# Sparse attention with a multiplicative feed-forward: w3 loaded ahead of batch 1, batch 1's phases in a new order, four stores on another queue

## Chip, cores and metric

The kernel runs on one core of one Trainium2 chip. The metric is the device time of one execution in microseconds (us). A profile of one further execution shows every instruction of the core's engines: PE (matrix products; PEld loads its weights), DVE, ACT and POOL (elementwise work), and SP, which here only issues transfers. Of these only PE, DVE, ACT and POOL compute.

## What is computed

`setup_inputs` draws q, k, v of 8 batches, 8 heads, 576 positions and 64 channels, and four weights; all are float32. Heads 0 to 3 attend to the last 32 positions, heads 4 to 7 to every 32nd position before. The result is projected twice, multiplied, and projected twice more.

```python
def _attn_ref(q, k, v):
    ...
    scores = scale * np.matmul(q, k.transpose(0, 1, 3, 2))
    ...
    mask_local = (rel >= 0) & (rel < stride)
    mask_strided = (rel >= 0) & (pos[None, :] % stride == pos[:, None] % stride)
    ...
    attn = attn / (np.sum(attn, axis=-1, keepdims=True) + 1e-09)
    return np.matmul(attn, v).astype(np.float32)

def _moe_ref(x, w1, w2, w3, w_out):
    a = x @ w1
    b = x @ w2
    h = a * b @ w3
    return (h @ w_out).astype(np.float32)
```

x has 4608 rows (8 times 576) and 512 columns; w1 and w2 are 512x1024, w3 1024x1024, w_out 1024x512.

## The kernel before

**Attention.** The 64 heads are 32 pairs, four to a batch: p0 to p3 are batch 0, p4 to p7 batch 1, p8 to p11 batch 2. Pairs 0 and 1 of a batch are local, 2 and 3 strided. A pair goes through these phases: T (PE transposes its q and k, ACT or DVE copy them from PSUM to `qT` and `kT`), S (scores on PE, exp on ACT, mask product on DVE), PV (product with v on PE, then `norm` on DVE: a reciprocal and a product), T2 (PE transposes the result, ACT and DVE copy it to `xT`). Batches 0 and 1 use the functions that begin with `ah_`, in two halves (groups 0 and 1) of a pair; later batches use `ph_`. `ah_R` transposes the last 64 positions of all pairs of a batch, and its second part (the tail) copies q's part for the strided pairs. Strided pairs of batches 0 and 1 have their probabilities in a large buffer `nptm`, which has to be cleared first (`nptm1` for batch 1), and a small DVE copy (`ah_tail`, L434) behind each mask product (`mask_mul`, L343).

**Feed-forward.** Rows are cut into nine tiles of 512. `ab_parts` makes a, b and their product for a tile (L585, L594, L597), `o_parts` the product with the folded weight (L635), whose result ACT copies to `osb` (L646, three buffers) and stores (L647). w3 and w_out are folded on the chip into `w34`: `fold_tr(jc)` transposes the jc-th 128 rows of w3 (L677), `fold_mm(jc)` multiplies them with w_out in two halves. Batch 1's last part of attention stands among these: 31 units are issued one after the other, and `plan` says behind which unit a phase of batch 1 is put. Units 1 to 23 are the fold (unit 14 is fold_tr(5), 15 and 16 the second half of fold 4 and the first of fold 5, 17 fold_tr(6), 18 and 19 halves of folds 5 and 6, 20 fold_tr(7), 21 to 23 halves of folds 6, 7 and 7), 24 to 31 the halves of tile 0's four products, each pair of which ends in a store. Then come the parts of tile 1 that belong to batch 0's last 64 rows (`over_parts`), and the loop over tiles, in which the later batches' attention is spread.

**Order of the work.** PE's instructions run in the order of the code. The other engines' and the queues' order is set when the kernel is built, from priorities in the order of the code and a model of when each instruction can start, so it can differ from the code's. All loads are issued by SyncE, all stores but one by ACT. Each load goes to one of nine staging buffers (`stgp`) and is then cast to float16 by POOL, so a load waits for the cast of the ninth load before it. The transposed pieces of w3 lie in six buffers (`w3n`): the seventh and eighth piece wait for fold_tr(0) and fold_tr(1). `load_vL` loads v of the local pairs in two halves (four transfers, L221, casts L222 and copies L91), `load_vN` and `load_vX` that of the strided pairs; `load_rest` the last 64 positions of q and k (L209); `load_qk(b, grp)` q and k of two pairs (L199).

**PSUM** has eight banks: psF three, psB two times two (`sps`, `pt`, `xps`), psM one, used by R, T2 and, before the change, by T of batch 1's local pairs. T of p6 and p7 takes two banks of psF.

Of the kernel before, what the change touches and what calls it, by code (L numbers as in the profile page):

```python
# [19 lines left out]
def kernel(  # L20
# [11 lines left out]
    nc = tc.nc  # L32
# [4 lines left out]
    P = 128  # L37
    NT = 512
    NTILE = NTOK // NT
    KM = DM // P  # L40
    KF = DF // P
# [33 lines left out]
    def pe(ins):  # L75
        return tc.keep_in_program_order(ins)
# [3 lines left out]
    def behind(ins):  # L80
        return tc.issue_after(ins.ins) if ins is not None else nullcontext()
# [4 lines left out]
    def copy(eng, out, in_):  # L86
        if eng == "a":
            return nc.scalar.copy(out=out, in_=in_)  # L88
        elif eng == "v":
            return nc.vector.tensor_copy(out=out, in_=in_)  # L90
        return nc.gpsimd.tensor_copy(out=out, in_=in_)  # L91
# [72 lines left out]
    out_r = out.rearrange("(c p) n -> c p n", p=P)  # L164
# [12 lines left out]
    def load_w3(jc, eng):  # L177
        st = stgp.tile([P, DF], FP32, tag="stg")
        nc.sync.dma_start(st, moe_w3[bass.ds(jc * P, P), :])
        t = ffn.tile([P, DF], FP16, tag="w3n", bufs=6)  # L180
        w3n[jc] = t
        copy(eng, t, st)
# [13 lines left out]
    def load_qk(b, grp, engs="pp"):  # L196
        for nm, ten, eng in (("q", q, engs[0]), ("k", k, engs[1])):
            st = stgp.tile([P, 4, 4, D], FP32, tag="stg")
            nc.sync.dma_start(st.rearrange("p h c d -> p h (c d)"),  # L199
                              ten[b, 4 * grp:4 * grp + 4, 0:NM].rearrange("h (p c) d -> p h (c d)", c=4))  # L200
            t = qkp.tile([P, 4, 4, D], FP16, tag=f"{nm}{grp}")
            with behind(setup["p"] if b == 0 and grp == 0 else None):
                copy(eng, t, st.rearrange("p h c d -> p c h d"))
            x16[(b, nm, grp)] = t
# [52 lines left out]
    for b in range(B):  # L257
        for hp in range(4):
            s = Pair()
# [107 lines left out]
    def ah_T1(s, i, dst=None):  # L367
        if dst is None:
            dst = psF.tile([P, 2 * NM], FP16, tag="f", name="tps")[:, 0:NM]
        src = x16[(s.b, "qk"[i], s.hp // 2)]  # L370
        h0 = 2 * (s.hp % 2)
        for c in range(4):
            pe(nc.tensor.transpose(dst[:, c * P:(c + 1) * P],
                                   src[:, c, h0:h0 + 2].rearrange("p h d -> p (h d)"), id16))
        return dst

    def ah_T1c(s, i, dst):
        t = (qT, kT)[i]
        eng = "v" if i and (s.b == 0 or not s.local) else "a"
        if s.local:  # L380
            copy(eng, t[:, s.hp, 0:NM].rearrange("x (p c) -> x p c", c=4),
                 dst.rearrange("x (c p) -> x p c", c=4))
        elif i:
            copy(eng, t[:, s.hp, 0:NM], dst)
        else:
            copy(eng, t[:, s.hp].rearrange("x (c w) -> x c w", w=NW)[:, :, 0:P],
                 dst.rearrange("x (c p) -> x c p", c=4))
# [2 lines left out]
        ah_T1c(s, i, ah_T1(s, i))  # L390

    def ah_T(s):
        if s.b and s.local:
            ps = psM.tile([P, 2, NM], FP16, tag="m", name="tps")
            pst = [ah_T1(s, i, ps[:, i]) for i in range(2)]
        else:
            pst = [ah_T1(s, i) for i in range(2)]
        for i in range(2):
            ah_T1c(s, i, pst[i])

    def ah_R(b):
        ps = psM.tile([P, 1024], FP16, tag="m", name="rps")
        pvs = [ps[:, 256 * i:256 * i + 256].rearrange("x (g a w) -> x g a w", g=2, a=2) for i in range(2)]
        src = x16[(b, "r")]
        for g in range(4):
            pe(nc.tensor.transpose(pvs[g // 2][:, g % 2].rearrange("x a w -> x (a w)"),
                                   src[:, 2 * g:2 * g + 2].rearrange("p h d -> p (h d)"), id16))
        for i, t in enumerate((qT, kT)):
            copy("av"[i], t[:, 0:2, NM:S], pvs[0][:, :, i])
        copy("v", kT[:, 2:4, NM:S], pvs[1][:, :, 1])  # L410

        def tail():
            copy("a" if b else "v", qT[:, 2:4].rearrange("x g (c w) -> x g c w", w=NW)[:, :, :, P:NW],
                 pvs[1][:, :, 0].rearrange("x g (j c) -> x g c j", c=4))

        return tail

    def ah_home(s):
        if s.nat:
            return nptms[s.b][:, s.hp - 2], NE  # L420
        return ptms[s.hp % 2], PTW

    def ah_off(s, g):
        return g * (640 if s.local else 2 * QN[2])
# [12 lines left out]
    def ah_group(s, g):  # L437
        m = s.n // 2
        e = s.n if g else m
        return range(g * m, e), s.q[g * m], s.q[e]  # L440
# [55 lines left out]
    def ah_PV(s, g):  # L496
        cs, lo, hi = ah_group(s, g)
        ptm, end = ah_home(s)
        if s.b == 0:
            xps = psF.tile([P, NB], FP32, tag="f", name="xpl")[:, 0:390].rearrange("p (h x) -> p h x", h=2)  # L500
        else:
            xps = psB.tile([P, 2, NB], FP32, tag="big", name="xps")
        for i, c in enumerate(cs):
            for h in range(2):
                c0 = ah_off(s, g) + h * (hi - lo) + s.q[c] - lo
                m = min(P, end - c0)
                o = xps[0:m, h, i * 65:(i + 1) * 65]
                tail = s.nat and c == NC
                pe(nc.tensor.matmul(o, ptm[0:s.kr, c0:c0 + m],
                                    s.v[0:s.kr, 2 * (s.hp % 2) + h, c, :], start=True, stop=not tail))  # L510
                for e in range(NC if tail else 0):
                    e0 = NE + h * 256 + e * 64
                    pe(nc.tensor.matmul(o, ptm[:, e0:e0 + P], s.v[:, 2 * (s.hp % 2) + h, e, :],
                                        start=False, stop=e == NC - 1))
        if g == 0:
            s.xqs = att.tile([P, LT, 2, D], FP16, tag="xqs", bufs=2, name="xqs")
        norm(s, xps[0:s.kr, :, 0:len(cs) * 65], cs[0], len(cs))

    def norm(s, xv, c0, l):
        w = s.kr  # L520
        rcp = att.tile([P, 2, LT], FP32, tag="rcp")
        xv = xv.rearrange("p h (i e) -> p h i e", e=65)
        nc.vector.reciprocal(out=rcp[0:w, :, 0:l], in_=xv[:, :, :, D])
        nc.vector.tensor_mul(s.xqs[0:w, c0:c0 + l].rearrange("p i h d -> p h i d"), xv[:, :, :, 0:D],  # L524
                             _ap(rcp, 0, [[rcp.ap[0][0], w], [LT, 2], [1, l], [0, D]]))
# [115 lines left out]
    def o_parts(tch):  # L641
        res = []
        for ts in range(NT // P):
            def done(ps, ts=ts):
                osb = ffn.tile([P, DM], FP32, tag="osb", bufs=3)
                nc.scalar.copy(out=osb, in_=ps)  # L646
                nc.scalar.dma_start(out_r[tch * (NT // P) + ts], osb)  # L647

            if tch + 1 < NTILE or ts + 1 < NT // P:
                res += acc_parts(lambda ci, ts=ts: abts[tch][:, ci, bass.ds(ts * P, P)],  # L650
                                 lambda ci: w34[:, ci, :], done, 4)
        return res
# [49 lines left out]
    def ph_TS(s, t):  # L702
        if s is not None:
            pt, soft = ph_S(s)
            after = [soft]
        else:
            pt = psB.tile([P, 2, NB], FP32, tag="big", name="pt")
            after = []
        if t is not None:
            after.append(ph_T(t, t.hp == 0, pt))  # L710
        for f in after:
            f()
# [116 lines left out]
    load_w3(0, "p")  # L829
    for g in range(4):  # L830
        load_wo(g, "p")
    for jc in range(1, 6):
        load_w3(jc, "p")
    load_qk(1, 0)
    load_w3(6, "p")
    load_rest(1)
    load_w3(7, "p")
    load_vL(1)
    load_qk(1, 1)
    load_vN(1)  # L840

    while pos[0] < batch_end[0]:
# [18 lines left out]
    p4, p5, p6, p7, p8 = pairs[4:9]  # L861
    def nptm1():
        nptms.append(ffn.tile([P, 2, 2048], FP16, tag="abt", bufs=4, name="nptm1"))
        clear(nc.vector, nptms[1])

    plan = ((24, nptm1), (15, ah_T, p4), (18, lambda: ah_R(1)()), (19, ah_T, p5), (20, ah_S, p4), (22, ah_S, p5),
            (23, ah_PV, p4, 0), (24, ah_PV, p4, 1), (25, ah_PV, p5, 0), (25, ph_T2, p4), (26, ah_PV, p5, 1),
            (26, ah_T, p6), (27, ah_T, p7), (28, ah_S, p6), (28, ph_T2, p5), (29, ah_S, p7), (30, ah_PV, p6, 0),
            (31, ah_PV, p6, 1), (31, ah_PV, p7, 0))
    for i, u in enumerate(units, 1):  # L870
        u()
        for x in plan:
# [4 lines left out]
    load_vX(2)  # L877
    over = over_parts()
    tile1 = ab_parts(1) + o_parts(1)
    for u in over[0:3]:  # L880
        u()
    ph_T2(p6)
    over[3]()
    ah_PV(p7, 1)
    over[4]()
    ph_TS(None, p8)
    for u in over[5:]:
        u()
    tile1[0]()
# [56 lines left out]
```

## Time and profile before

| what | value |
|---|---|
| median of 3 runs | 278.85 us (275.86, 278.85, 280.79) |
| profiled execution | 277.33 us, span 275.6 us from the first to the last instruction |
| PE / DVE / ACT / POOL busy | 259.7 / 150.4 / 146.7 / 100.3 us |
| PE's granted clock | 0.998 |
| moved by DMA | 48.66 MB, 177 GB/s in the mean |

Busy times are sums over the span and don't add up, since engines work at the same time. A line of a timeline has the start, the length, the engine, the line of the kernel, the operation and its tiles, and in square brackets the idle time of that engine just before it with what ended it. "ACTq" and "SPq" are the issuing of transfers by ACT and SyncE. A line of waits has who waited for whom, the sum in us, how often, and the longest.

### The profile page before, as it was taken

Reading aid. Unit: us, or ns where it says so; the run is one execution under the profiler, and the core shown is the slowest. Engines: PE = TensorE matmul, PEld = TensorE weight load, DVE = VectorE, ACT = ScalarE, POOL = GpSimd, SP = SyncE. Lnnn points to the kernel's source line nnn. Section 1 sums busy time; section 2 is a strip of 40 time slices with the busy share of each in tenths; the row PEclk is TensorE's granted clock in tenths of the full one; section 3 lists DMA queues with packets and bytes.
Section 4 is the critical chain, followed back from the end, with each engine's and each line's share of the span. In section 5 each row is a group of like instructions: output and inputs, shape, how many; then the busy total and the mean of one; then the engine's idle time right before and its main releaser. Section 6 shows DMA issues by size and latency. Waiting matters only on the chain.

```text
span 275.6 us, 6430 instructions
## 1 busy us (share of the span) xinstructions
PE 259.7 (94%) x2508; PEld 138.3 (50%) x2508; DVE 150.4 (55%) x340; ACT 146.7 (53%) x304; POOL 100.3 (36%) x119
## 2 busy tenths in 40 slices
PE   2989999987789999999999999999999999999995
PEld 1654445543645555555555555555555544444442
DVE  7483533483877547755775576467547752431430
ACT  2754334737356765657555565656665664324322
POOL 5577785765446533557248275200000000000000
PEclk9999999999999999999999999999999999999999
DMA  7999999998599749499596994210021012003004
GB/s 213 289 353 394 394 386 249 252 247 249 188 234 229 218 159 273 135 244 305 150 263 188 288 236 146 100 54 4 2 114 40 0 40 114 0 4 150 0 1 153
DMA packets 61099, 48.66 MB, mean 177 GB/s; under 512 B 31804, under 2 KB 52492, under 8 KB 61068
## 3 DMA queue, kind: packets, MB, share of 16 engines
q1 hardware_dynamic: 55884, 38.87, 51.1%
q10 hardware_dynamic: 5184, 9.37, 9.0%
q8 instruction: 19, 0.31, 0.5%
q14 instruction: 12, 0.10, 0.1%
HBM read 38.80 MB, written 9.44 MB: 175 GB/s over the span
## 4 chain that ended last, share of the span: by engine, by line
PE 76%; DMA 10%; DVE 5%; ACT 3%; SPq 2%; issue 1%; ACTq 1%; POOL 1%; POOLq 0%
PE ops L635 23%; PE aps L585 20%; PE bps L594 19%; DMA st<-in_moe_w_dram 8%; PE sps L363 3%; PE ps L533 3%; DMA st<-in_v_dram 2%; PE sps L329 2%; PE pt L286 2%; DVE ptm L343 1%; PE pt L329 1%; PE trp L677 1%; ACT qT L88 1%; ACTq L647 1%; SPq L199 1%
## 5 line engine op out<-in xcount | busy, mean ns | idle before, releaser
L594 PE MATMUL bps<-xT,w2h 128*128 128x512 f16 (+1 forms) x288 | 74.7, 376 | 0.0
L585 PE MATMUL aps<-xT,w1h 128*128 128x512 f16 (+1 forms) x288 | 73.6, 377 | 0.5 <-ACT xT L540 0.5
L635 PE MATMUL ops<-w,abt 128*128 128x512 f16 x280 | 67.0, 379 | 0.0
L597 DVE TENSOR_TENSOR abt<-bps,asb 128x512 f16<-128x512 f32 (+1 forms) x72 | 48.8, 680 | 32.0 <-PE bps L594 29.6
L565 ACT COPY asb<-aps 128x512 f32<-128x512 f32 (+1 forms) x72 | 42.5, 593 | 43.0 <-PE aps L585 40.6
L91 POOL CAST t<-st 128x1024 f16<-128x1024 f32 (+1 forms) x46 | 48.2, 1055 | 33.1 <-DMA st<-in_k_dram 12.4
L585 PEld LDWEIGHTS <-w1h 128*128 128x128 f16 x288 | 26.4, 98 | 29.6 <-issue 1.0
L594 PEld LDWEIGHTS <-w2h 128*128 128x128 f16 x288 | 26.1, 98 | 26.4 <-issue 0.3
L635 PEld LDWEIGHTS <-abt 128*128 128x128 f16 x280 | 25.2, 98 | 26.0 <-issue 0.2
L354 ACT ACTIVATE pte<-sps 128x1024 f16<-128x1024 f32 (+1 forms) x24 | 24.6, 1026 | 11.4 <-PE sps L329 11.4
L646 ACT COPY osb<-ops 128x512 f32<-128x512 f32 x35 | 20.6, 589 | 17.2 <-PE ops L635 17.2
L524 DVE TENSOR_TENSOR xqs<-sps,rcp 128x768 f16<-128x768 f32 (+1 forms) x24 | 21.4, 891 | 0.8
L343 DVE TENSOR_TENSOR ptm<-pte,maskL 128x1152 f16<-128x1152 f16 (+2 forms) x16 | 12.9, 808 | 14.4 <-ACT pte L354 13.6
L88 ACT COPY qT<-pt 128x224 f16<-128x224 f16 (+4 forms) x60 | 18.0, 361 | 3.5 <-ACT osb L646 1.6
L343 DVE TENSOR_TENSOR ptm<-pte,maskX 126x1152 f16<-126x1152 f16 x12 | 10.2, 848 | 13.4 <-ACT pte L354 13.4
L222 POOL CAST v16L<-st 96x768 f16<-96x768 f32 x16 | 13.2, 824 | 10.0 <-DMA st<-in_v_dram 7.2
L545 ACT COPY xT<-ps 128x504 f16<-128x504 f16 x12 | 6.9, 578 | 18.3 <-PE ps L533 18.3
L250 POOL CAST v16X<-st 126x1024 f16<-126x1024 f32 x6 | 6.8, 1129 | 24.4 <-DMA st<-in_v_dram 17.6
L635 PE MATMUL ops<-woh,w3T 128*128 128x512 f16 x64 | 15.6, 380 | 0.0
L533 PEld LDWEIGHTS <-xqs 96*128 96x128 f16 (+3 forms) x176 | 11.5, 97 | 8.1 <-DVE xqs L524 1.9
L533 PE MATMUL ps<-id,xqs 96*128 96x96 f16 (+3 forms) x176 | 14.1, 210 | 1.2 <-DVE xqs L524 1.2
L90 DVE COPY kT<-pt 128x512 f16<-128x512 f16 (+4 forms) x48 | 14.1, 324 | 1.4 <-ACT kT L88 0.6
(114 smaller groups left out, 265.7 us busy)
## 6 DMA issues: line engine op xcount, KB each, us to landing
out_dram<-osb ACTq DMA_DIRECT2D x35, 256.0 KB
st<-in_q_dram SPq DMA_DIRECT2D x16, 512.0 KB
st<-in_k_dram SPq DMA_DIRECT2D x16, 512.0 KB
st<-in_moe_w_dram SPq DMA_DIRECT2D x16, 512.0 KB
st<-in_v_dram SPq DMA_DIRECT2D x32, 144.0 KB
st<-in_v_dram SPq DMA_DIRECT2D x24, 112.0 KB
st<-in_moe_w_out_dram SPq DMA_DIRECT2D x4, 512.0 KB
st<-in_q_dram SPq DMA_DIRECT2D x8, 128.0 KB
```

Of the source, the lines that this page charges most:

```text
L88: return nc.scalar.copy(out=out, in_=in_)
L91: return nc.gpsimd.tensor_copy(out=out, in_=in_)
L343: nc.vector.tensor_mul(o.rearrange("p (a x) -> p a x", x=x), i.rearrange("p (a x) -> p a x", x=x), _ap(s.mask, lo, [[s.mask.ap[0][0], s.kr ...
L354: nc.scalar.activation(out=pv[0:kr, :, lo:hi], in_=src, func=AF.Exp, bias=0.0, scale=scale)
L524: nc.vector.tensor_mul(s.xqs[0:w, c0:c0 + l].rearrange("p i h d -> p h i d"), xv[:, :, :, 0:D], _ap(rcp, 0, [[rcp.ap[0][0], w], [LT, 2], [ ...
L533: pe(nc.tensor.transpose(ps[:, o:o + l], s.xqs[0:l, t].rearrange("p h d -> p (h d)"), id16[0:l, 0:l]))
L565: nc.scalar.copy(out=st["asb"][:, 0:nt], in_=st["a"][:, 0:nt])
L585: pe(nc.tensor.matmul(st["a"][:, 0:nt], w1h[:, ci, bass.ds(jc * P, P)], xT[ci][:, tok], start=(ci == 0), stop=(ci == KM - 1)))
L594: pe(nc.tensor.matmul(st["b"][:, 0:nt], w2h[:, ci, bass.ds(jc * P, P)], xT[ci][:, tok], start=(ci == 0), stop=(ci == KM - 1)))
L597: nc.vector.tensor_mul(abts[tch][:, jc, skip:], st["b"][:, 0:nt], st["asb"][:, 0:nt])
L635: pe(nc.tensor.matmul(st["ps"], lhs(ci), rhs(ci), start=(ci == 0), stop=(ci == KF - 1)))
L646: nc.scalar.copy(out=osb, in_=ps)
```

## The change

It has four parts. (1) All eight pieces of w3 are loaded ahead of batch 1; both halves of batch 1's q and k come ahead of its v. (2) T of all pairs of batch 1 uses one bank of psM. (3) The phases of batch 1 have new places in `plan`, p6's and p7's T and p6's S ahead of PV of p4, and behind the units T of p8 comes first, ahead of the overflow parts and PV of p7's second half. (4) The four stores of tile 0 are issued by SyncE; in the code they stand ahead of `load_vL(2)`, `load_qk(2, 1)` and `load_vX(2)`.

```diff
     def ah_T(s):
-        if s.b and s.local:
+        if s.b:
             ps = psM.tile([P, 2, NM], FP16, tag="m", name="tps")
...
                 nc.scalar.copy(out=osb, in_=ps)
-                nc.scalar.dma_start(out_r[tch * (NT // P) + ts], osb)
+                (nc.scalar if tch else nc.sync).dma_start(out_r[tch * (NT // P) + ts], osb)
...
-    for jc in range(1, 6):
+    for jc in range(1, KF):
         load_w3(jc, "p")
     load_qk(1, 0)
-    load_w3(6, "p")
     load_rest(1)
-    load_w3(7, "p")
+    load_qk(1, 1)
     load_vL(1)
-    load_qk(1, 1)
     load_vN(1)
...
-    plan = ((24, nptm1), (15, ah_T, p4), (18, lambda: ah_R(1)()), (19, ah_T, p5), (20, ah_S, p4), (22, ah_S, p5),
-            (23, ah_PV, p4, 0), (24, ah_PV, p4, 1), (25, ah_PV, p5, 0), (25, ph_T2, p4), (26, ah_PV, p5, 1),
-            (26, ah_T, p6), (27, ah_T, p7), (28, ah_S, p6), (28, ph_T2, p5), (29, ah_S, p7), (30, ah_PV, p6, 0),
-            (31, ah_PV, p6, 1), (31, ah_PV, p7, 0))
+    plan = ((16, ah_T, p4), (18, lambda: ah_R(1)()), (19, ah_T, p5), (20, ah_S, p4), (21, ah_T, p6), (22, ah_S, p5),
+            (23, ah_T, p7), (23, nptm1), (24, ah_S, p6), (25, ah_PV, p4, 0), (25, ah_PV, p4, 1), (26, ah_PV, p5, 0),
+            (27, ah_S, p7), (27, ah_PV, p5, 1), (27, ph_T2, p4), (28, ph_T2, p5), (29, ah_PV, p6, 0),
+            (30, ah_PV, p6, 1), (31, ah_PV, p7, 0))
...
-    for u in over[0:3]:
+    ph_TS(None, p8)
+    over[0]()
+    ah_PV(p7, 1)
+    for u in over[1:4]:
         u()
     ph_T2(p6)
-    over[3]()
-    ah_PV(p7, 1)
     over[4]()
-    ph_TS(None, p8)
     for u in over[5:]:
```

## Prediction

> **What bounds the kernel now.** I read the page first, then PE's waits, then PE's busy time in stretches of the middle, then the timelines of ACT, POOL, DVE and SyncE there.
>
> ```profile
> PE 259.7 (94%) x2508; PEld 138.3 (50%) x2508; DVE 150.4 (55%) x340; ACT 146.7 (53%) x304; POOL 100.3 (36%) x119
> ...
> PE   2989999987789999999999999999999999999995
> ```
>
> PE is busy for 94% of the span. The only slices below 9 after the start are slices 9 to 11, about 55 to 76 us. After that PE is full to the end, so a microsecond saved before 78 us is a microsecond off the span, and none can be saved behind it. PE's busy time in stretches (length, PE, PEld, DVE, ACT, POOL):
>
> ```profile
> 46.00:52.00 6.00, 5.48 (x52) 3.46 (x50) 1.89 (x5) 3.45 (x8) 3.78 (x5) 1.00 1.05 205
> 52.00:58.00 6.00, 5.79 (x59) 2.78 (x56) 4.89 (x10) 4.33 (x9) 4.86 (x6) 1.00 1.04 321
> 58.00:64.00 6.00, 3.89 (x44) 2.51 (x45) 3.04 (x9) 2.42 (x5) 3.67 (x6) 1.00 0.88 176
> 64.00:71.00 7.00, 5.88 (x73) 2.91 (x72) 4.68 (x11) 4.40 (x8) 4.58 (x7) 1.00 0.89 282
> 71.00:77.50 6.50, 5.01 (x142) 4.09 (x138) 4.67 (x16) 2.87 (x9) 1.34 (x2) 1.00 0.41 130
> ```
>
> 31.5 us hold 26.05 us of PE work: 5.5 us idle, all that the change can win. A matmul's shown end overlaps the next one's start (four 128x512 show 1.03 us but follow each other every 0.86), so each of some six gaps hides about 0.1 more: I count 6.1 from start to start. PE's waits in that stretch say what ended them:
>
> ```profile
> PE tps L373 <- ACT qT L88: 1.8, 2, 1.3
> PE xps L509 <- DVE xqs L524: 1.8, 2, 1.0
> PE ps L533 <- DVE xqs L524: 1.0, 2, 0.8
> ```
>
> The 1.3 is batch 1's transposes of p7 at 63.26. They wait for the copy of p6's q, which stands on ACT behind a store's issue:
>
> ```profile
> 59.62 0.64 ACT L88 COPY xT<-ps 128x576 f16<-128x576 f16 x1 [1.21 <-PE ps L533]
> 59.98 2.60 ACTq L647 DMA_DIRECT2D out_dram<-osb  x1
> 62.63 0.58 ACT L88 COPY qT<-tps 128x512 f16<-128x512 f16 x1 [2.37 <-PE ops L635]
> ```
>
> The DVE waits are p4's to p7's softmax, norm and next bank of psB, one after the other, late because p6 and p7 begin only at 60.5. Batch 1's loads set how early they could begin (POOL's casts: w3's sixth, q, k of p4/p5, w3's seventh and eighth, k of p6/p7):
>
> ```profile
> 40.71 1.04 POOL L91 CAST t<-st 128x1024 f16<-128x1024 f32 x1 [0.26 <-DMA st<-in_moe_w_dram]
> 42.22 1.04 POOL L91 CAST t<-st 128x1024 f16<-128x1024 f32 x1 [0.47 <-DMA st<-in_q_dram]
> 44.24 1.04 POOL L91 CAST t<-st 128x1024 f16<-128x1024 f32 x1 [0.99 <-DMA st<-in_k_dram]
> 46.32 1.04 POOL L91 CAST t<-st 128x1024 f16<-128x1024 f32 x1 [1.04 <-DMA st<-in_moe_w_dram]
> ...
> 49.81 1.04 POOL L91 CAST t<-st 128x1024 f16<-128x1024 f32 x1 [1.47 <-PE rps L406]
> ...
> 55.98 1.58 POOL L91 CAST t<-st 128x1024 f16<-128x1024 f32 x1 [0.69 <-DMA st<-in_k_dram]
> ```
>
> **Loads.** No transfer is added; SyncE issues the same ones and POOL makes the same casts in another order. From 28 to 42 us DMA is full, and one 512 KB piece of w3 follows the other every 1.28 us (35.57 to 40.71 is four). So the two moved pieces come at 42.0 and 43.3. Their buffers are free: fold_tr(0) and (1) read the old ones at 36.7 and 39.0. q and k of p4/p5 move 2.57 later: cast from 44.8 and 46.8, the k done at 47.85. The rest (before: 47.72) now has one more piece ahead of it: about 49.0, cast (0.61) done at 49.6. k of p6/p7 no longer has four 144 KB transfers of v ahead: 0.59 MB at the 265 GB/s of 49 to 56 us is 2.2 us, at the 188 of the slice in which v's short rows move 3.1. So it lands at 53.0 (52.9 to 53.8) and is cast by 54.1 to 54.6. The v's are cast some 2 to 3 us later, by about 57.5 instead of 54.1. p4's PV wants its half at 59.
>
> **PE walked in the new order.** Unit 15 ends at 46.84 as before.
> - Unit 16 to 47.70. T p4 (0.45) now stands here; its k half waits for the cast of 47.85: 0.2 idle (0 to 0.5). Its cover of 1.5 us in the old order is gone.
> - fold_tr, half a fold, R at 49.6, unit 19, T p5. T p5 waits for R's last copy out of the one psM bank, as now: 0.5 idle. S p4 starts at about 52.05, where it starts now.
> - Unit 21 to 53.3, T p6: its k half would start at 53.5 and waits for the cast: 0.6 idle (0 to 1.5).
> - Unit 22, S p5, unit 23, T p7 at about 56.4. Both T now use psM, one bank: q's copy on ACT, then k's on DVE, then the next T. p6's copies fit in by 55.9 (DVE: mask 0.65, cast 0.68, copy 0.41). No store stands on ACT: the 1.3 us wait is gone. nptm1's clear costs nothing by its new place: it takes woh's buffer and so starts behind unit 23 in both orders (55.55 now).
> - Unit 24, S p6, unit 25, PV p4 twice to 59.5, unit 26 to 60.4. PV p5 needs p4's norm (0.18 + 0.56, starts 0.7 apart), on DVE behind p6's two mask products and two tails.
>
> ```profile
> 65.73 0.46 DVE L343 TENSOR_TENSOR nptm<-pte,maskN 128x576 f16<-128x576 f16 x1 [1.40 <-ACT pte L490]
> 66.22 0.24 DVE L434 COPY nptm<-nptm 128x64 f16<-128x64 f16 x1
> ...
> 67.96 0.98 DVE L343 TENSOR_TENSOR nptm<-pte,maskN 128x576 f16<-128x576 f16 x1 [0.78 <-ACT pte L490]
> 68.98 0.65 DVE L434 COPY nptm<-nptm 128x64 f16<-128x64 f16 x1
> ```
>
> The same product takes 0.46 or 0.98, the tail 0.24 to 0.97; POOL worked during the slow ones. Masks run from 58.75: done with norm at 61.0 if quick, at 62.6 if slow; idle 0.6 to 2.2, I take 1.0, since POOL is then busy 60% (3.67 of 6 us). The Trainium skill's page SBUF — State Buffer, section Who interferes with whom, says that a DVE instruction with two SBUF inputs and a GpSimd instruction that reads SBUF exclude one another, and the later one blocks; the two durations agree, and if every product met a whole 1.04 us cast, this step would be at its slow end.
> - S p7 and PV p5's second half each want a bank of psB freed by norm or exp: 0.6 (0 to 1.0).
> - Units 28 to 31 and p6's PV end at about 69; p8's transposes, the overflow parts and PV p7 then cover each other: of the 1.5 us of waits from 71 to 77.5, 0.1 stays (0 to 0.5).
>
> **Stores.** SyncE now waits in line for four copies of osb. Behind them stand batch 2's v (4 issues), q and k of p10/p11, and v of its strided heads (10); POOL casts them and PE's PV p8 and T p10 wait for those. ACT loses 2.60 + 3 x 0.34 us of issues. Store 3 is ready at 69.3. For the v behind it the nearest row with an idle queue is a rest: issued from 100.51, cast at 105.41, 4.9 us. So v is cast from 74.2 to 75.8 (0.82 + 0.71), and PV p8 wants it at 76.0. q and k issue 3.8 us later and are cast behind both v's, k by about 80. T p10 wants it at 79.6. I take 0.5 idle; 0 if v's rows flow faster, 1.5 if they take the 6.5 us of 101.91 to 108.37. The 2.60 us issue overlaps SyncE's four v issues (57.09 to 63.11); the other three take 0.34 in ACT's line. The Trainium skill's Perfetto Trace Analysis, section DMA Instruction — HWDGE, holds that a DMA waits inside its profiled time for a shared descriptor generator; by that the store costs SyncE about 0.34, by the row alone 2.60, 2.3 us more for all behind it.
>
> **Sum.** 0.2 + 0.5 + 0.6 + 1.0 + 0.6 + 0.1 + 0.5 = 3.5 us stay of 6.1: 2.6 us less. The profiled execution took 277.33 (span 275.6 and 1.7 around it): 274.7. The times I have are 275.86, 277.33, 278.85, 280.79; the middle is 278.1, so I predict 275.5. A step of 2% is 5.6 us, about what this kernel's scatter lets one tell from no change.
>
> **Rivals.**
> - *DVE and the late k become the limit* (gain 0.5, 277.6). T p6 waits 1.1 (k cast at 54.6), PV p5 2.2, S p7 and PV p5's second half 1.0; with the other four terms as summed 5.6 of 6.1 stay. For it: the 0.98 rows, and k's cast of 1.58. Against: POOL has less to do from 62 on, as v is cast later.
> - *Everything is covered* (gain 5.1, 273.0): T p5's 0.5 and some 0.5 of bank waits stay. Against: psM has one bank for all seven T, R and T2 steps.
> - *Batch 2's values come too late* (slower, about 279.2). Store 3's issue takes 2.60 (+2.3), and v 6.5 us (+1.6): v is cast at 79.7, PV p8 idles 3.7 instead of the 0.5 and, with q and k also queued, T p10 0.5 more: 0.5 + 3.7 = 4.2 against 0.5, which turns -2.6 into +1.1. It decides once v comes 3 us after PV p8 wants it. For it: SyncE's queue is in order. Against: stores meet an empty queue there, and such issues took 0.34.
> - *SyncE doesn't get that order.* The order on ACT isn't the code's: p4's exp runs at 52.68 ahead of the w3T copy (53.27) that the code has first. If v is placed between the stores, the 0.5 falls away: gain 3.1, 275.0.
>
> **How the numbers follow.** Forecast 0.45 (own range 274.2 to 276.8), DVE and k 0.22, values late 0.13, all covered 0.10, other order 0.10. The range takes the covered case (273.0) less some scatter at one end and the late values (279.2) at the other: 272.4 to 279.3. Faster by over 2% needs the covered case and a favourable draw: 0.07. Slower by over 2% (over 283.7) needs the late values at twice their price: 0.05.
>
> **What would show it.** Right: the 2.60 us issue is gone from ACT; T p6 and T p7 lie near 54 and 56; PE's busy slices 9 and 10 rise to 9; the first full stretch (L594 behind p9's transposes, now 77.49) begins near 74.9. PE waits for a POOL cast at T p6 and for DVE at PV p5. Wrong: PE waits for v16L at PV p8, or the slices fill and the span stays, which would mean that PE is not what sets the end after 78 us.

## Result, and the profile after

The changed kernel takes 275.62 us in the median of 20 runs (273.66 to 279.88); the kernel before, in 20 runs beside it, 277.8 us (275.86 to 281.18). The ratio is 0.9909 (95% interval 0.9887 to 0.9931): some 2.5 us, a gain of 0.9%, well inside the 2% that count as no change. Forecast were 275.5 us and 2.6 us less.

About half of this gain is a matter of PE's clock. In the profiled executions a mean granted clock of 0.994 or less goes with a stretch of 3.4 us or more at half clock: four of the fourteen have it (0.987 to 0.994, the first profile after, e3, e5 and e12), the ten at 0.998 or more have no such stretch. Beside `e1_again` the kernel before was at 0.998 or more in only 12 of 33 runs, with a median of 276.57 us; the changed kernel was so in 9 of 12, with 275.19: 1.4 us less (95% interval 0.7 to 2.5). The other 1.2 us come from the kernel before having its clock lowered more often. Why it does so is not shown, since its one trace, at 0.998, has no such stretch. Below, "at full clock" means runs at 0.998 or more. The profiled execution before, 277.33, lies near the upper end of the full-clock runs (275.76 to 277.87), so the two profiles differ by more than the typical 1.4 us.

The first profiled execution of the changed kernel took 278.06 us: its fold waited 1.98 us for a piece of w3 that landed late and then ran at half clock (told at the end). So the lines below are from a second one, of the same kernel unmodified, which took 275.19 us (run `e1_again`).

The head of the page, shares of the span and PE's slices:

```profile
PE 259.4 (95%) x2508; PEld 138.6 (51%) x2508; DVE 151.6 (55%) x340; ACT 146.5 (54%) x304; POOL 100.3 (37%) x119
...
PE   2979999897999999999999999999999999999995
```

PE's work is the same (259.4 us against 259.7), the span is 273.3 us instead of 275.6. Counted from 1, slices 9, 11 and 12, which were 8, 7 and 8, are 9 now; slice 10 is still 7, slice 8 has become 8. Two of the same five stretches as before (length, PE, PEld, DVE, ACT, POOL; then clock, and DMA's share and GB/s):

```profile
58.00:64.00 6.00, 5.12 (x53) 2.41 (x52) 4.82 (x12) 2.67 (x5) 3.88 (x5) 1.00 0.75 178
...
71.00:77.50 6.50, 6.15 (x131) 4.54 (x128) 4.31 (x13) 4.71 (x13) 1.47 (x2) 1.00 0.68 203
```

Over all five PE is busy for 28.7 of the 31.5 us, before for 26.05: 2.7 us less idle, of which 1.2 come from 58 to 64 and 1.1 from 71 to 77.5. PE's waits in this stretch:

```profile
PE xps L509 <- DVE xqs L524: 0.8, 1, 0.8
PE xps L509 <- ACT pte L490: 0.8, 1, 0.8
PE tps L373 <- ACT qT L88: 0.6, 1, 0.6
PE sps L363 <- DVE ptm L343: 0.4, 1, 0.4
PE tps L373 <- POOL t L91: 0.2, 1, 0.2
```

The 1.3 us behind ACT's store is gone; what stays is PV p5 twice (0.84 for p4's norm, 0.76 for an exp), T p5, PV p8 and T p4. The first full stretch begins at 74.77, instead of 77.49.

### The profile page after: what moved, and what is told of

It is laid out like the page before. It is cut to its first block, busy times and chain, and to the rows that moved or that the text cites. A ratio compares the mean times of both kernels' runs of the same rounds, so it can differ in the third digit from the quotient of the medians.

```text
span 276.3 us, 6424 instructions
## 1 busy us (share of the span) xinstructions
PE 260.3 (94%) x2508; PEld 139.1 (50%) x2508; DVE 150.4 (54%) x340; ACT 146.3 (53%) x304; POOL 98.8 (36%) x119
## 4 chain that ended last, share of the span: by engine, by line
PE 80%; DMA 10%; DVE 2%; SPq 2%; ACT 2%; POOL 1%; issue 0%; POOLq 0%
PE ops L635 26%; PE aps L585 20%; PE bps L594 19%; DMA st<-in_moe_w_dram 8%; PE sps L363 3%; PE ps L533 3%; DMA st<-in_v_dram 2%; PE pt L286 2%; PE sps L329 2%; PE pt L329 1%; SPq L199 1%; PE trp L677 1%; DVE nptm L343 1%; PE tps L373 1%; DVE nptm L434 1%; POOL v16L L222 1%
## 5 line engine op out<-in xcount | busy, mean ns | idle before, releaser
L91 POOL CAST t<-st 128x1024 f16<-128x1024 f32 (+1 forms) x46 | 45.7, 998 | 38.7 <-DMA st<-in_q_dram 19.7
L343 DVE TENSOR_TENSOR ptm<-pte,maskL 128x1152 f16<-128x1152 f16 (+2 forms) x16 | 12.2, 767 | 13.7 <-ACT pte L354 12.8
L635 PE MATMUL ops<-woh,w3T 128*128 128x512 f16 x64 | 17.3, 410 | 0.0
L363 PEld LDWEIGHTS <-ptm 128*128 128x128 f16 (+1 forms) x264 | 11.2, 97 | 6.1 <-DVE ptm L343 1.4
```

The lines of the kernel that those rows point to most:

```text
L343: nc.vector.tensor_mul(o.rearrange("p (a x) -> p a x", x=x), i.rearrange("p (a x) -> p a x", x=x), _ap(s.mask, lo, [[s.mask.ap[0][0], s.kr ...
L363: pe(nc.tensor.matmul(s.ps[:, h, c * 65:c * 65 + 65], s.ptm[0:s.kr, c0:c0 + P], s.v[0:s.kr, 2 * (s.hp % 2) + h, c, :], start=True, stop=True))
L635: pe(nc.tensor.matmul(st["ps"], lhs(ci), rhs(ci), start=(ci == 0), stop=(ci == KF - 1)))
```

## Experiments

Theory: the gain is the one that the sum says, the loads let p6 and p7 begin early and the stores' move takes ACT's stall away, each worth something. Rivals: the stores alone bring it, the loads alone bring it, or the new places do. The table has, for each kernel, the ratio to the kernel before with its 95% interval, the median, the median at full clock with the number of such runs (the kernel before: 276.57, 12 of 33, beside e1 to e4; 276.40, 9 of 23, beside e5 to e8; 276.44, 14 of 23, beside e9 to e12), and from the profiled execution where the first full stretch begins and how far that is behind the fold's second group of transposes (L677; before: at 77.49, 40.8 behind those at 36.67).

| kernel | ratio | median us | at full clock | full stretch at | behind the fold |
|---|---|---|---|---|---|
| e1_again (the change) | 0.9924 (0.9886 to 0.9962) | 275.26 | 275.19 (9 of 12) | 74.77 | 37.3 |
| e2_act_stores | 0.9927 (0.9897 to 0.9958) | 275.74 | 275.64 (11 of 12) | 75.09 | 38.8 |
| e3_old_loads | 1.0015 (0.9976 to 1.0054) | 278.40 | 275.91 (3 of 12) | 78.86 | 42.0 |
| e4_stores_only | 0.9907 (0.9873 to 0.9941) | 275.00 | 274.85 (9 of 10) | 74.66 | 37.5 |
| e5_loads_only | 1.0001 (0.9961 to 1.0040) | 277.86 | 277.62 (8 of 12) | 78.83 | 41.2 |
| e6_v_first | 0.9848 (0.9800 to 0.9896) | 274.34 | 274.34 (6 of 6) | 74.00 | 36.9 |
| e7_all_behind | 0.9928 (0.9891 to 0.9965) | 276.66 | 276.10 (10 of 12) | 74.00 | 37.6 |
| e8_replan | 0.9807 (0.9764 to 0.9849) | 273.29 | 273.29 (6 of 6) | 72.99 | 36.3 |
| e9_no_casts | 1.0010 (0.9975 to 1.0045) | 276.76 | 276.46 (9 of 11) | 77.09 | 40.1 |
| e10_replan_five | 0.9894 (0.9855 to 0.9933) | 273.44 | 273.42 (5 of 6) | 73.52 | 36.7 |
| e11_small | 0.9963 (0.9933 to 0.9993) | 275.67 | 275.67 (9 of 12) | 74.09 | 37.8 |
| e12_replan_again | 0.9901 (0.9864 to 0.9938) | 273.94 | 273.90 (5 of 6) | 74.68 | 36.2 |

When the fold begins hangs on when w3 lands, which scatters by more than 1 us from execution to execution; a late start is partly regained behind it, so neither of the last two columns is exact, and the waits are the finer evidence. The ratio takes in runs with the clock lowered too, of which the kernel before has the most. e9 had a twelfth run, of 932.5 us, that its full-clock median leaves out.

**The change again, without an edit** (e1_again).

> The changed kernel as it is, for a profile in which nothing ahead of the change is late (in the one at hand w3's first pieces came 2 us late, PE idled 2.0 us at fold_tr(1) and its granted clock was 0.5 for 3.4 us after that). Theory A (the prediction's): 2.5 us less than before (ratio 0.991); between 46 us and the first full stretch PE idles some 3 to 3.5 us, at T p5 (0.5 to 0.6), at T p4 or T p6 for POOL's casts (together 0.2 to 1.0), at PV p5's first half for DVE's norm (1.0 to 1.7), at PV p5's second half for an exp (0.5 to 0.8). Rival B (all loads are early enough): no wait for a cast at T p4 and T p6, as in the profile at hand, and the first full stretch begins 0.6 us earlier than A says.

Shown above.

**The change without the stores' move** (e2_act_stores).

```diff
-                (nc.scalar if tch else nc.sync).dma_start(out_r[tch * (NT // P) + ts], osb)
+                nc.scalar.dma_start(out_r[tch * (NT // P) + ts], osb)
```

> The changed kernel with tile 0's four stores issued by ACT again. Theory A (the parts pay together; the store's issue is long on ACT only while SyncE issues v's short rows): the first store is issued near 60 us, where SyncE issues batch 2's v, and takes 1 to 2.6 us on ACT; exp of p7 or a copy of osb stands behind it, so 0.5 to 1.5 us of the gain of 2.5 are lost: ratio 0.993 to 0.997 to before. Rival C (the store's move is the whole gain): ratio 1.000 within 0.002. Rival D (the new places alone took p6's and p7's T out of the store's way): no loss, ratio 0.991.

ACT's timeline has the long issue again, at the same time:

```profile
59.63 2.87 ACTq L647 DMA_DIRECT2D out_dram<-osb  x1
```

Yet the median is 275.74, within the scatter of the change itself. In the new order T p7 already lies ahead of this issue, and nothing that PE wants soon stands behind it: ACT's next copy waits for PE in any case. Three waits grew in this execution, by 1.6 us together (PV p5's first half 1.50 instead of 0.84, T2 p5 0.55 instead of none, PV p8 0.71 instead of 0.35), but they stand behind DVE products that POOL's casts stretched: p6's first mask took 1.17 us (0.46 in e1_again), p7's first 1.06 (0.46), p8's 1.11 (0.76). ACT, then DVE, then POOL:

```profile
63.13 0.59 ACT L646 COPY osb<-ops 128x512 f32<-128x512 f32 x1 [3.52 <-PE ops L635]
...
58.51 1.17 DVE L343 TENSOR_TENSOR nptm<-pte,maskN 128x576 f16<-128x576 f16 x1 [0.62 <-ACT pte L490]
...
58.33 1.04 POOL L91 CAST t<-st 128x1024 f16<-128x1024 f32 x1
```

So the issue itself costs nothing that can be seen here. With the stores on ACT, SyncE issues v from 55.22 on, and the casts lie earlier.

**The change with the loads in the old order** (e3_old_loads).

```diff
-    for jc in range(1, KF):
+    for jc in range(1, 6):
         load_w3(jc, "p")
     load_qk(1, 0)
+    load_w3(6, "p")
     load_rest(1)
-    load_qk(1, 1)
+    load_w3(7, "p")
     load_vL(1)
+    load_qk(1, 1)
```

> The changed kernel with the loads in the old order (two pieces of w3 behind q and k of p4/p5, v ahead of q and k of p6/p7). Theory A: k of p6/p7 is cast by 57.5 as before, T p6 wants it at 53.5, so PE idles 3.5 to 4 us there in the place of up to 0.6; T p4 loses its 0.2. The gain is lost and more: 0.5 to 1 us slower than before, ratio 1.002 to 1.004. Rival E (the loads don't matter since DVE's chain has slack of its own behind T p6): PE idles at T p6, but less at PV p5, and the ratio is 0.993 to 0.997.

PE's timeline:

```profile
55.33 0.40 PE L373 MATMUL tps<-id,t 128*128 128x128 f16 x4 [1.60 <-POOL t L91]
57.09 0.61 PE L373 MATMUL tps<-id,t 128*128 128x128 f16 x4 [1.37 <-POOL t L91]
```

T p6 in its new place waits 2.97 us in two steps for the casts of q and k, and from 55.8 to 62.6 the granted clock is 0.51, which costs PE up to 3.4 us more (told at the end). The whole gain is gone from the median: the loads have to move for the phases to move. Nine of the twelve runs had the clock lowered; the other three have a median of 275.91, too few to say how much of the loss is the clock's and how much the waits'.

**The stores' move alone** (e4_stores_only: the kernel before with the one line of part 4).

```diff
-                nc.scalar.dma_start(out_r[tch * (NT // P) + ts], osb)
+                (nc.scalar if tch else nc.sync).dma_start(out_r[tch * (NT // P) + ts], osb)
```

> The kernel before with only the four stores moved to SyncE. Theory A: the wait of 1.3 us at T p7 goes, and what stands behind it in DVE's and PE's chain comes 1 to 1.3 us earlier; the waits at PV p5 (1.0), at p6's PV and T2 (1.0 and 0.8) stay: ratio 0.995 to 0.997. Rival C (the store is the whole gain): ratio 0.991. Rival F (what stands on ACT behind the store is not what p7 waits for): ratio 1.000.

The ratio is 0.9907, as with all four parts; at full clock 274.85, 1.7 us below the kernel before (0.6 to 2.0). PE's timeline (T p6, then T p7):

```profile
60.36 0.61 PE L373 MATMUL tps<-id,t 128*128 128x128 f16 x8
61.67 0.61 PE L373 MATMUL tps<-id,t 128*128 128x128 f16 x8
```

T p7 waits for nothing (1.32 us before). T p6 is where it was, at 60.4. Still the waits for `xqs`, 1.8 and 1.0 us before, have shrunk. Before, two of them lay ahead of the store's issue or beside it (0.81 at 58.59, 0.20 at 59.29) and two behind it (0.96 at 70.17, 0.84 at 72.56). Here they are 0.19, 0.20, 0.31 and none. The two behind it, before, and the one that is left in e4:

```profile
70.17 0.33 PE L509 MATMUL xps<-v16X,nptm 128*128 128x65 f16 x5 [0.96 <-DVE xqs L524]
72.56 0.32 PE L533 MATMUL ps<-id,xqs 128*128 128x128 f16 x3 [0.84 <-DVE xqs L524]
...
68.71 0.30 PE L509 MATMUL xps<-v16X,nptm 128*128 128x65 f16 x4 [0.31 <-DVE xqs L524]
```

With 0.23 new at an `osb` copy and 0.28 at PV p8, PE is busy for 28.96 of the 31.5 us from 46 to 77.5, 2.9 more than before: 1.3 for T p7, 1.5 for the two waits behind it, 0.6 for the one ahead of it, less 0.5. SyncE's timeline shows that nothing takes the stall's place:

```profile
58.94 0.37 SPq L647 DMA_DIRECT2D out_dram<-osb  x1
59.41 0.38 SPq L221 DMA_DIRECT2D st<-in_v_dram  x1
```

The store takes 0.37 us there, and batch 2's v begins behind it.

**The loads' move alone** (e5_loads_only: the kernel before with the load order of part 1).

```diff
-    for jc in range(1, 6):
+    for jc in range(1, KF):
         load_w3(jc, "p")
     load_qk(1, 0)
-    load_w3(6, "p")
     load_rest(1)
-    load_w3(7, "p")
-    load_vL(1)
     load_qk(1, 1)
+    load_vL(1)
```

> The kernel before with the changed kernel's loads, old places, stores on ACT. Measure: the time from fold_tr(1)'s first transpose to the first full stretch of PE (L594 behind p9's transposes), 40.8 us in before, 37.3 changed, 37.5 with the stores alone moved. Theory A: T p4, in its old place behind unit 15, waits 0.6 to 1.1 us for the cast of k (it had 1.5 us of cover and k comes 2.6 us later); T p6 and T p7 stand where they stood, so nothing is won: 40.8 to 41.8, ratio 1.000 to 1.004. Rival G (the loads alone relieve POOL and DVE): 39.5 to 40, ratio 0.996.

Ratio 1.0001: nothing in the median, and at full clock it is slower, 277.62 against 276.40 (0.2 to 1.7 us more). ACT's line and then PE's, T p7:

```profile
60.52 3.38 ACTq L647 DMA_DIRECT2D out_dram<-osb  x1
...
64.58 0.61 PE L373 MATMUL tps<-id,t 128*128 128x128 f16 x8 [2.10 <-ACT qT L88]
```

The store's issue is longer than before (3.38 us), T p7 waits 2.10 instead of 1.32, and the clock is 0.5 for 3.4 us behind it, 1.7 us lost; the half-speed matmuls also cover waits that would else show, so this trace says little about the DVE waits.

**v of batch 2 ahead of the stores** (e6_v_first: e4, and `load_vL(2)` placed ahead of the units).

```diff
+    load_vL(2)
     plan = ...
...
-    load_vL(2)
     load_qk(2, 1)
```

> The kernel before with the stores on SyncE, but batch 2's local v loaded ahead of all four, as early as before. It parts two ways in which the stores' move can win. Theory H (ACT's stall was the loss): all of the gain stays: 37.5 us from fold_tr(1) to the full stretch, ratio 0.991. Theory I (half of it comes from holding v back, whose casts on POOL then no longer meet the mask products and tails of p6 and p7 on DVE: 0.88 to 0.98 and 0.65 to 0.97 in before, mostly 0.46 to 0.52 and 0.24 with the stores moved): T p7's wait of 1.3 us is gone but the waits of 0.8 to 1.0 at p6's PV and T2 come back: 38.5 to 39.5, ratio 0.994 to 0.997.

SyncE's timeline:

```profile
55.09 5.12 SPq L221 DMA_DIRECT2D st<-in_v_dram  x4
60.31 5.94 SPq L647 DMA_DIRECT2D out_dram<-osb  x3
```

v is issued in one piece, the first store behind it takes 0.66 us, T p7 doesn't wait. So the long issue is not the store's own work. On four kernels (before, e2, e5, e9) ACT's first store took 2.60, 2.87, 3.38 and 4.03 us; on SyncE the first one took 0.37 and 0.66. What makes it long stays open. SyncE issuing v at the same time is not enough: before, two later stores on ACT took 0.34 each while SyncE issued v of the strided heads. Nor does it need to go on: in e5 v's issue ended at 60.45, and ACT's long one began at 60.52. ACT and SyncE before, then SyncE in e5:

```profile
67.40 0.34 ACTq L647 DMA_DIRECT2D out_dram<-osb  x1
65.64 5.34 SPq L241 DMA_DIRECT2D sy<-in_v_dram  x4
...
55.50 4.95 SPq L221 DMA_DIRECT2D st<-in_v_dram  x4
```

A store on ACT that fell among the four short-row issues of L221 took 0.34 as well (e4 at 98.87, e2 at 100.43). That it is ACT's first store is not enough either: in e4 the first one on ACT, at 92.30, took 0.38. The Trainium skill's page Perfetto Trace Analysis, section DMA Instruction — HWDGE (DVE, Sync), has a DMA instruction wait inside its profiled time for the shared descriptor generator. The four long rows would fit that, the rows of 0.34 beside v's issue don't follow from it, and which resource is shared isn't shown.

POOL's v casts now lie at 62.5 to 66.5 and stretch DVE's tails behind p6's masks to 0.75 and 0.65, while p7's masks run at 0.46 and 0.49. The median, 274.34, is 0.2% below e4's; the two ratios' intervals overlap.

**All of batch 2's loads held behind the fourth store** (e7_all_behind).

```diff
+                setup["st"] = (nc.scalar if tch else nc.sync).dma_start(...)
...
-    load_vL(2)
-    load_qk(2, 1)
-    load_vX(2)
+    with behind(setup["st"]):
+        load_vL(2)
+        load_qk(2, 1)
+        load_vX(2)
```

> The changed kernel with all of batch 2's v and its second q and k held behind the fourth store on SyncE, which is the order that the prediction took (in the changed kernel v stands between the stores). The prediction: PE idles 0 to 1.5 us for v at PV p8 or for k at T p10, 0.5 taken: ratio 0.993, 37.3 us to the full stretch, and one new wait of PE for a POOL cast behind it. Its rival (values too late): 3 us and more, ratio 1.002 or above. Rival J (v flows fast into an empty queue): no wait, ratio 0.991.

This is the order that the prediction had priced. SyncE, then PE:

```profile
59.86 10.26 SPq L647 DMA_DIRECT2D out_dram<-osb  x4
70.21 3.03 SPq L221 DMA_DIRECT2D st<-in_v_dram  x4
...
76.80 0.53 PE L363 MATMUL sps<-v16L,ptm 128*128 128x65 f16 x12 [1.11 <-DVE kT L90]
80.64 0.29 PE L286 MATMUL pt<-id,t 64*128 64x64 f16 x8 [0.31 <-POOL t L91]
```

v's last POOL copy ends at 76.74 in this execution, 0.06 before PV p8, so it is v that PE waits for, not the DVE copy that the line names. 0.76 more than the 0.35 of the change, and 0.31 at T p10: 1.1 us for what was priced at 0.5, inside 0 to 1.5. The median, 276.66, is 1.4 above e1_again's, at full clock 0.9, but the two intervals of the ratio overlap wholly.

**Without POOL's casts of batch 2's v and second q, k** (e9_no_casts: the kernel before; the casts are left out, and the second q, k of batch 1 used in their place).

```diff
-    load_vL(2)
-    load_qk(2, 1)
+    load_vL(2, cast=False)
+    load_qk(2, 1, cast=False)
```

> The kernel before, stores on ACT, with POOL's casts of batch 2's local v and of its second q and k left out (their transfers stay; batch 2 then computes with other values that lie there). That leaves ACT's stall as it is and takes away the casts that meet DVE's mask products and tails of p7. Theory H (ACT's stall is the loss and drags the rest along): T p7 still waits 1.3 us, 40.8 us from fold_tr(1) to the full stretch become at best 40.3, ratio 0.998 to 1.000. Theory I (POOL's contention is half of it): p7's products fall from 0.98 to about 0.5 and its tails from 0.65 and 0.97 to 0.24, 1.5 to 2 us of chain: 38.8 to 39.5, ratio 0.993 to 0.995.

DVE's lines of p7's first mask and tail (0.98 and 0.65 before):

```profile
69.37 0.46 DVE L348 TENSOR_TENSOR nptm<-pte,maskN 128x576 f16<-128x576 f16 x1 [0.78 <-ACT pte L495]
69.86 0.24 DVE L439 COPY nptm<-nptm 128x64 f16<-128x64 f16 x1
```

So POOL's casts do double them. PE's two waits behind the stall (0.96 and 0.84 before) are gone, although the stall is longer: the store's issue took 4.03 us and T p7 waited 2.75, 1.43 more than before. SyncE goes on sooner here (the next q is issued at 61.55, before at 63.22); that this lengthens the store's issue is a guess. The two changes cancel, and the time is the same. With e4, where the stall is gone and the casts stay (p6's second tail 0.91, p7's mask 0.88) and these waits are 0.31 and none, this says that they need both: a DVE already late, and casts that stretch what it does.

**A version that goes further** (e8_replan: the change, with T p5 behind unit 20, p6's second mask product and its tail, `m6[1]`, held on DVE until p4's last norm product, `p4.last`, is done, and PV p5's second half and T2 of p5 a unit later; e12_replan_again is the same kernel once more).

```diff
+    def m6_1():
+        with behind(p4.last):
+            m6[1]()
...
-    plan = (..., (19, ah_T, p5), ..., (24, ah_S, p6), (25, ah_PV, p4, 0), (25, ah_PV, p4, 1), (26, ah_PV, p5, 0),
-            (27, ah_S, p7), (27, ah_PV, p5, 1), (27, ph_T2, p4), (28, ph_T2, p5), ...
+    plan = (..., (20, ah_T, p5), ..., (24, ah_S, p6, m6), (24, lambda: m6[0]()), (25, ah_PV, p4, 0),
+            (25, ah_PV, p4, 1), (25, m6_1), (26, ah_PV, p5, 0), (27, ah_S, p7), (27, ph_T2, p4), (28, ah_PV, p5, 1),
+            (29, ph_T2, p5), ...
```

> The changed kernel with three places moved against its remaining waits: T p5 one unit later (its wait of 0.59 for R's copies), the second mask product of p6 on DVE behind p4's norms (PV p5's first half waits 0.84 for them), PV p5's second half one unit later, behind T2 of p4 (it waits 0.76 for p7's exp). Theory A: these waits are what is left, and they go without others in their place: 37.3 becomes 35.5 to 36.0, ratio 0.984 to 0.987 to before. Rival K (a chain on DVE of norms, masks and tails is full and sets the pace from p6's scores to PV p7): the waits move to p6's PV, T2 p5 or T8, 36.7 to 37.3, ratio 0.989 to 0.992.

> The kernel with the three moved places once more, for the comparison on one chip with the fifth pair and with the small edit. 0.981 was measured; from its profile (36.3 us to the full stretch, 1 us less than the changed kernel) 0.987 is what the waits account for. Expected: 0.981 to 0.987.

Of e8's waits in the middle these stay above 0.3 us:

```profile
PE sps L450 <- DVE xqs L530: 0.4, 1, 0.4
PE sps L363 <- DVE ptm L343: 0.4, 1, 0.4
PE xps L515 <- DVE xqs L530: 0.3, 1, 0.3
```

T p5's 0.59 is gone, PV p5 waits 0.34 instead of 0.84 and 0.76, S p7 0.45 new; PE is busy for 29.96 of the same 31.5 us. So PV p5's wait was what the prediction had made it: p4's norm behind p6's masks. The two runs gave 0.9807 and 0.9901, intervals that don't touch; their medians, 273.29 and 273.94, lie closer (0.24%) than the two medians of the kernel before that they are set against (277.88 and 276.98). Those differ by the clock: at full clock they are 276.40 and 276.44, and e8 and e12 lie 3.1 and 2.5 us below. With e10 the three medians are 0.5 to 0.8% below the change's 275.26 to 275.62; this is the best version here, about 1% below the kernel before at full clock. e6, with two lines changed, is 1.05 us behind e8 beside it on the same chip.

**Two more tries on top.** e10_replan_five is e8 with a fifth pair of parts of tile 1 ahead of PV p8, to cover its 0.35; e11_small is e6 with T p5 behind unit 20 and that fifth pair.

```diff
-    for i in (2, 1, 3, 5):
+    for i in (2, 1, 3, 5, 6):
...
-        tile1 = tile1[6:]
+        tile1 = tile1[7:]
```

> The changed kernel with the three moved places of the run before (T p5, p6's second mask product, PV p5's second half), and one more pair of products ahead of PV p8 (five in the place of four), since PE waits 0.35 us there for the mask product. That wait goes and nothing else changes: 0.3 to 0.4 us less than without the fifth; ratio 0.980 to 0.984. If the wait of PV p8 only moves to the next one (PV p9), nothing is won.

> The kernel before with old loads and old places, but the stores on SyncE behind batch 2's local v, T p5 one unit later and the fifth pair ahead of PV p8: the smallest edit that takes away the waits which the profiles name. Expected from 36.9 us with the stores behind v: T p5's 0.53 and PV p8's 0.59 go: 36.4 to the full stretch, and 0.5 less behind it; ratio 0.981 to 0.984, no worse than the kernel with new loads and new places. Rival: the new places have a lower floor, then it stays 0.3 % or more behind the other one of this call.

Neither clearly won. In e10 the wait moved: the added pair itself wants a copy by ACT (`asb`), and PE waits 0.47 for that at 75.67 instead of 0.35 for p8's mask. In e11 PE came early enough to wait 0.46 at PV p4 for the cast of batch 1's v, besides 0.42 at PV p5; 275.67 is not below e6's 274.34.

## Why the prediction came out, and where its steps did not

The total came out: 2.6 us were forecast, the ratio makes it 2.5, the full stretch came at 74.77 (forecast 74.9), and PE's listed idle time fell by 2.7. Part of this is luck. At full clock the gain is 1.4 us. The rest is a lowered clock that the kernel before has more often, a term that the sum doesn't have; the starting time, 278.1, was the middle of four times of which two, 278.85 and 280.79, lie above every full-clock run of that kernel (the highest is 277.87).

In the traces, too, an error and an accident met. The sum's own row (1.03 us shown, 0.86 apart) hides some 0.17 behind each gap, not 0.1, and the stretch before has nine gaps, not six: with 5.45 us listed, an estimate of 7.0 from start to start, not 6.1. In e1_again five gaps of 2.71 us listed make 3.6 in the same way, so some 3.4 us were won there, not 2.6. But the fold began 0.8 us later in that execution (37.47, not 36.67), and so the full stretch came only 2.7 earlier. And more of the total came from one part, the stores, than the prediction gave it. The waits, as the profile lists them:

| term | predicted us | in e1_again |
|---|---|---|
| T p4, k's cast | 0.2 | 0.17 |
| T p5, one bank of psM | 0.5 | 0.59 |
| T p6, k's cast | 0.6 | 0 |
| PV p5, first half | 1.0 | 0.84 |
| S p7, PV p5 second half | 0.6 | 0.76 |
| p8's transposes, overflow | 0.1 | 0 |
| stores: PV p8, T p10 | 0.5 | 0.35, by p8's mask |
| sum | 3.5 | 2.71 |

- T p6: the cast of k was done before the 54.1 to 54.6 of the estimate, and PE reached T p6 at 54.51 rather than 53.5, since its fold began 0.8 us later than in the kernel before. POOL's cast of k ran from 52.43 to 53.47. (The late end of the estimate was itself short: 53.8 and 1.04 make 54.8.) So the sign "PE waits for a POOL cast at T p6" stayed out, and so did half of another: PE's slice 9 rose to 9, slice 10 stayed at 7, where PV p5's two waits now lie.
- The stores: the rival "SyncE doesn't get that order" (0.10) is what happened. SyncE's timeline of the first profiled execution of the changed kernel has v between the stores:

```profile
63.32 0.38 SPq L647 DMA_DIRECT2D out_dram<-osb  x1
63.79 2.53 SPq L221 DMA_DIRECT2D st<-in_v_dram  x2
67.61 0.37 SPq L647 DMA_DIRECT2D out_dram<-osb  x1
68.07 1.01 SPq L221 DMA_DIRECT2D st<-in_v_dram  x2
71.69 0.36 SPq L647 DMA_DIRECT2D out_dram<-osb  x1
```

  PV p8's 0.35 is p8's mask on DVE (76.00, 0.76 long), not v. The rival in which values come too late needed 4.2 us of idle time; with the strict order forced (e7) it was 1.1, so that rival falls even on its own terms.
- The step that failed is the reading of the DVE waits as "late because p6 and p7 begin only at 60.5". In e4 T p6 stands at 60.4 and these waits all but vanish, with only the store's issue taken from ACT. Two of them stood behind that issue and went with it (or with the casts, e9); the 0.81 at 58.59 lies ahead of it, and is 0.19 in e4, 0.42 in e9 and absent in e6. Why that one shrinks was not separated from scatter. The prediction gave the stores' part the 1.3 us of one wait; alone it was worth the whole gain.
- Hence the parts don't add. Stores alone bring 0.93%, loads and places alone 0.73%, all together 0.76 to 0.91%; at full clock 1.7, 0.9 and 1.4 us. Either keeps T p7 from standing behind the long issue (in e2 it lies ahead of it), and that can be saved once. The new plan then pays 1.6 us at PV p5, where the old one with the stores moved (e4) waits 0.19; e8 gets most of it back.

## What to carry to other kernels

Look for the issue of a transfer in the line of a compute engine that lasts several times its usual length: moving that one instruction to the other queue may be worth more than the wait that names it, since everything behind it on the engine moves too. When several parts of a change remove the same wait, undo and do each alone before any is credited; here one line had all of the gain when tried alone, and the rest of the change was only worth having with a further repair of its own new wait. A reordering of phases moves the loads' due times as well: without its loads the new plan lost all it had won in the median. And look at the clock of each run before a gain is put down to waits: here it made about half of it.

## Not expected of the hardware

A wait of PE can cost more than itself. In the first profiled execution of the changed kernel, PE:

```profile
38.74 0.62 PE L677 MATMUL trp<-id,t 128*128 128x128 f16 x8 [1.98 <-POOL t L91]
39.19 3.56 PE L635 MATMUL ops<-woh,w3T 128*128 128x512 f16 x8
```

The eight products take 3.56 us; at the 0.86 from start to start for four of them it would be 1.7. The granted clock from 38.7 to 42.1 was 0.58, so behind the wait of 1.98 some 1.5 us more were lost. The same stands behind the 2.10 us wait in e5, behind 1.60 and 1.37 us in e3 (twice as long), and in e12 behind 1.14 us in a stretch with other idle time just ahead (from 18.7 to 22.1, clock 0.57). But e9's wait of 2.75 us was followed by a clock of 1.00, and so was e2's 1.50. So the length of the wait alone doesn't decide. The Trainium skill's page TensorE: Matmul & The Clock Gate, section Why this matters for your kernels, says that there should be no gap over about 3 us, one idle window, between bursts of matmuls: the stretches at half clock here, of 3.4 us or twice that, followed gaps well under 3 us. What decides was not tried, and so it stays open, too, why the kernel before has its clock lowered in more of its runs (21 of 33 beside e1_again) than e2 (1 of 12), e4 (1 of 10), e6 or e8 (none of 6 each). A wait of PE may set it off in those runs too, but no trace of such a run of the kernel before was kept, and e5 and e9, whose traces have the longest waits at T p7, had their clock lowered in only 4 of 12 and 2 of 11.
